# Attention, gated MLP and expert attention on one core: trace durations and nearly equal leanings for the scheduler behind the first attention

## The chip, the cores and the metric

The kernel runs on one core of one Trainium2 chip. The metric is device microseconds of one execution, the median over runs on the chip. TensorE (PE in the profile) multiplies matrices, VectorE (DVE), ScalarE (ACT) and GpSimd (POOL) work element by element, and SyncE (SP) issues transfers.

## The reference

Three parts follow one another, each on the output of the part before (numpy, shortened):

```
# 1: causal attention, 2 batches x 12 heads, 448 rows, 64 wide
attn = softmax(where(mask, -1e9, q @ k.T / 8));  x = attn @ v        # -> (2, 448, 768)
# 2: gated MLP
h = gelu(x @ w_in);  u, v = h[..., :512], h[..., 512:]
v_n = (v - mean) / sqrt(var + 1e-6) * g_ln
v_s = einsum('ts,bsd->btd', w_sg, v_n) + b_sg[None, :, None]
x2 = x + (u * v_s) @ w_out
# 3: four experts, each a causal attention of one head, two of them used per row
w = softmax of the two largest of x2 @ w_gate
for e in range(4):
    q, k, v = x2 @ wq[e], x2 @ wk[e], x2 @ wv[e]
    out += (e chosen) * w_e * (softmax(mask(q @ k.T / 8)) @ v @ wo[e])
```

## The kernel before

Most products are made from values split in two parts, a rounded high part and the remainder (names ending in h and l: gh and gl, xh and xl, wqh and wql). One product is then three matmuls, h by h, l by h and h by l (`mm3`, L820, and `u_chain`, L859). A split is two element-wise steps: a cast or copy that makes the high part (lines L371 on ScalarE, L373 on VectorE, L375 on GpSimd, all in one helper) and a subtraction that makes the remainder (L378, on VectorE or GpSimd). A name such as gl0_3 is the remainder of batch 0, block 3.

The first attention ends near 112 us of the span with the last products with v (L497). Behind it the parts overlap in time. `v_chain` makes v (gelu, layernorm; L990 to L1005), `spatial` multiplies by w_sg (L1053, eight blocks: 2 batches x 4 blocks f of 128 columns) and makes g: scale and bias on VectorE (L1056), the product with u (L1059), then the split into gh and gl. `wout_chain` multiplies g by w_out, 12 matmuls for each of 2 x 6 blocks d, adds x (L1074 the high part, L1077 the low part) and splits the sum into xh and xl. Then come the weights and projections of part 3 (v, then q and k for two pairs of experts in each batch; the pair's results are copied out of the accumulators as q30, k30, q31, k31, L371 or L373). `scores3` (L1302) makes the scores, `bank_chain` (L427, L437, L471, L473) the exponentials and their split as pn, a transposing transfer (L476, issued by SyncE, sixteen in all) turns pn into pt, `out_chain` multiplies pt by the values v3s (L516, L518, L520) and scales the result (r: L531, L533, L536; y: L541 on VectorE in one step, or L543 on ScalarE followed by L547 on GpSimd), `y_split` transposes y (L557) and splits it, and `wo_chain` (L1341) makes the output rows, which leave by transfers.

The order is not written by hand. The class `Order` plans it when the program is built: each part is a chain of steps, a step has a cost in ns for every engine that may do it, and `begin` works out for each engine the time at which the step could start. It picks the engine whose start + cost + leaning is least. The leaning is a constant per engine (`BIAS`; behind planned time 190000 ns `LATE`), to which a kind of step may add its own. `run` then takes, over all chains, the step that starts first, with ties within 60 ns broken by a rank (`R`). The instructions are issued on each engine in the order so planned, and the costs and leanings are nothing but plan: on the chip, an engine does its own instructions in this order, each as soon as what it needs is there. Costs come from the small functions `act` (ScalarE), `mm` (a matmul), `vec` and `vec2` (VectorE), `pool1` and `pool2` (GpSimd), L63 to L82, and from numbers written at single steps (for instance L425, L434, L989, L994, L1002, L1054).

The two lines that decide between engines:

```
bias = self.LATE[e] if t > self.TURN else self.BIAS[e] * min(1.0, t / 20000)
best = (t + c + bias, t, e, t + c)      # the least of these over the engines
```

Of the kernel before, what the change touches and what calls it, by code (L numbers as in the profile page):

```python
# [22 lines left out]
HF = 512  # L23
# [34 lines left out]

def act(n, sb=True, ap=False):
    return (94 if sb else 51) + 93 * ap + n / 1.2


def mm(n):
    return 2 + n / 2.4


def vec(n):
    return 69 + n / 0.96  # L70


def vec2(n):
    return 69 + n / 1.92


def pool1(n):
    return 56 + n / 0.96


def pool2(n):
    return 150 + 2.1 * n  # L82


class Step:
# [25 lines left out]
class Order:  # L111
# [10 lines left out]
    }  # L122

    BIAS = dict(T=0, A=300, V=800, G=-400, S=0, Z=0)
    LATE = dict(T=0, A=300, V=700, G=-300, S=0, Z=0)
    TURN = 190000

    def __init__(self):
        self.clock = dict.fromkeys("TAVGSZ", 600.0)
# [65 lines left out]
    def begin(self, ch):  # L195

        st = ch[4]
        for m in st.need:
            if m not in self.marks:
                return None  # L200
        items = []
        for r in st.take:
            name = r if isinstance(r, str) else r[0]
            free = [x for x in self.rings[name] if not any(x is y for y in items)]
            if not free or (name != r and self.held[r[:2]] + st.take.count(r) > r[2]):
                return None
            items.append(min(free, key=lambda x: x[0]))
        best = None
        for e, c in st.cost.items():

            t = ch[5] if st.dma and ch[3] == "D" else ch[2] + self.delay(ch[3], e)
            t = max(self.clock[e], t)
            for m in st.need:
                t = max(t, self.marks[m][0] + self.delay(self.marks[m][1], e))
            for x in items:
                t = max(t, x[0] + self.delay(x[1], e))
            if st.dma:
                t = max(t, self.hw)
            if e == "T" and not self.warm(t):
                c *= 2  # L220
            bias = self.LATE[e] if t > self.TURN else self.BIAS[e] * min(1.0, t / 20000)
            bias += st.bias.get(e, 0)
            if best is None or t + c + bias < best[0]:
                best = (t + c + bias, t, e, t + c)
        return best[2], best[1], items, best[3]
# [67 lines left out]
def attention_moe_kernel(  # L293
# [19 lines left out]
    o = Order()  # L313
    done, give = o.done, o.give

    uid = [0]

    def nm(s):
# [68 lines left out]
        return dict(A=act(n, False), V=vec(n))  # L387

    def subs(n):
        return dict(V=vec(n), G=pool2(n))  # L390


    class Core:
# [23 lines left out]
    def bank_chain(c, key, bank, s, pts, pt_of=None):  # L417

        parts = []
        for i in BANKS[bank]:  # L420
            _, c0, n = PLACE[i]

            parts.append((i, slice(0, 64 if i == 0 else P), slice(c0, c0 + n)))

        _, tm, bias = yield op(V=690, take=("tm" + c.n, "bias" + c.n))  # L425
        for i, rs, cs in parts:
            V.tensor_tensor_reduce(  # L427
                out=tm[rs, cs], in0=s[rs, cs], in1=masks[i][rs], scale=-0.125, scalar=3.0e38,
                op0=ALU.add, op1=ALU.min, accum_out=bias[rs, i : i + 1],
            )  # L430
        give(BS, s)
        if not c.split:
            _, p32, sm = yield op(A=1000, take=("p32" + c.n, "sm" + c.n))
        else:  # L434
            _, p32 = yield op(A=800, take=("p32" + c.n,))
        for n, (i, rs, cs) in enumerate(parts):
            A.activation(p32[rs, cs], tm[rs, cs], AF.Exp, bias=bias[rs, i : i + 1], scale=-1.0,  # L437
                         **({} if c.split else dict(accum_out=sm[rs, n : n + 1])))
        give("tm" + c.n, tm)
        give("bias" + c.n, bias)  # L440
        if not c.split:
            yield op(G=230)
            G.tensor_scalar(sm[:, 0:2], sm[:, 0:2], 1.0, 1e-9, op0=ALU.mult, op1=ALU.add)
            yield op(V=160)
            V.reciprocal(sm[:, 0:2], sm[:, 0:2])  # L445
            e, = yield op(kind="pr", G=950, V=500)
            for n, (i, rs, cs) in enumerate(parts):
                if e == "V":
                    V.tensor_scalar(p32[rs, cs], p32[rs, cs], sm[rs, n : n + 1], None, op0=ALU.mult)  # L449
                else:  # L450
                    G.tensor_scalar(p32[rs, cs], p32[rs, cs], sm[rs, n : n + 1], 0.0, op0=ALU.mult, op1=ALU.add)  # L451
            give("sm" + c.n, sm)
            _, t = yield op(T=440, take=(BT,))
            for blk, to in enumerate(SLOTS[bank]):
                T.transpose(t[:, to * P : to * P + P], p32[:, blk * P : blk * P + P], ident)  # L455
            give("p32" + c.n, p32)
            pt = yield from pt_of()
            e, = yield Step(copies_ps(512), kind="pt")
            copy(e, pt.rearrange("p (a s) q -> p a s q", s=4)[:, :, 2 * bank : 2 * bank + 2, :],
                 t.rearrange("p (a s q) -> p a s q", a=2, s=2))  # L460
            give(BT, t)
            pts["pt"] = pt
            done(("p", key, bank))
            return
        e, pn = yield Step(copies(512), ("pn" + c.n,), kind="hi")
        if e == "A":
            A.mul(pn[:, :512], p32, PSC)
        elif e == "V":
            V.tensor_scalar(pn[:, :512], p32, PSC, None, op0=ALU.mult)
        else:  # L470
            G.tensor_scalar(pn[:, :512], p32, PSC, 0.0, op0=ALU.mult, op1=ALU.add)  # L471
        yield op(V=vec(512))
        V.scalar_tensor_tensor(pn[:, 512:], p32, PSC, pn[:, :512], op0=ALU.mult, op1=ALU.subtract)  # L473
        give("p32" + c.n, p32)
        _, pt = yield dma_t(896, ("pt" + c.n,))
        nc.sync.dma_start_transpose(pt, pn)  # L476
        give("pn" + c.n, pn)
        pts[bank] = pt
        done(("p", key, bank))
# [446 lines left out]

    def open_c2():
        yield wait(*[("x", b, c) for b in range(B) for c in range(NC)])
        s1_stack.close()
        s3a = ctx.enter_context(tc.tile_pool(name="s3a", bufs=1, side="right"))  # L930
        for c in range(NC):
            wvh.append(ct([P, NV], F32R, f"wvh{c}", s3a))
            wvl.append(ct([P, NV], F32R, f"wvl{c}", s3a))
        c2 = c2_stack.enter_context(tc.tile_pool(name="c2", bufs=1, side="right"))
        for b in range(B):

            vn[b] += [ct([P, HF], F32, f"vn{b}_{j}", c2) for j in range(4)] if b == 0 else []
        vn[1] += [vn[0][0], *[ct([P, HF], F32, f"vn1_{j}", c2) for j in range(1, 4)]]
        for c in range(4):
            wsg.append(ct([P, SG], F32, f"wsg{c}", c2))  # L940

        wsg[0] = [wsg[0], ct([P, SG], F32, "wsg0b", c2)]
        for t, rows in zip(wsg[0], (LOW, TOP)):
            G.memset(t[rows], 0.0)
        u2[1] = [ct([P, S], F32, f"u2_1_{f}", c2) for f in range(4)]
        done("c2")
        for c in range(4):
            o.add(R["sgt"] + c, sg_chain(c))
# [30 lines left out]
    def v_chain(b, j):  # L979
# [6 lines left out]
        _, v2 = yield Step({"Z": 0}, ("big",))  # L986
        yield from gelu2(v2, o_, HF, v2)
        give(BC, o_)
        _, m = yield op(V=602, take=("mv",))  # L989
        V.bn_stats(m[:, 0:6], v2)  # L990
        yield op(V=75)
        V.bn_aggr(m[:, 6:8], m[:, 0:6])

        yield op(G=1120)  # L994
        G.tensor_scalar(m[:, 8:9], m[:, 6:7], -1.0, 0.0, op0=ALU.mult, op1=ALU.add)
        G.tensor_scalar(m[:, 7:8], m[:, 7:8], 1.0, 4e-6, op0=ALU.mult, op1=ALU.add)
        G.tensor_tensor(m[:, 7:8], m[:, 7:8], nhalf, op=ALU.pow)
        G.tensor_mul(m[:, 8:9], m[:, 8:9], m[:, 7:8])
        yield wait("c2")
        e, = yield op(V=456, A=act(HF, ap=True) + 100)  # L1000
        x = vn[b][j]
        if e == "V":  # L1002
            V.tensor_scalar(x, v2, m[:, 6:7], m[:, 7:8], op0=ALU.subtract, op1=ALU.mult)
# [38 lines left out]
    def spatial(b, f):  # L1042
        fs = slice(f * P, f * P + P)

        ts_ = slice(64, SG) if b == 0 else slice(0, S)
        _, t = yield op(T=4 * mm(S), take=(BC,),
                        need=["halves", *[("vn", b, j) for j in range(1, 4)], *[("sg", c) for c in range(4)], ("u", b, f)])
        for j in range(4):
            if j:
                yield op(T=4 * mm(S), need=[("vn", b, 0)] if j == 3 else ())  # L1050

            i, w = (j + 1, wsg[j + 1]) if j < 3 else (0, wsg[0][b])
            T.matmul(t[:, :S], lhsT=vn[b][i][:, fs], rhs=w[:, ts_], start=(j == 0), stop=(j == 3))  # L1053
        _, g0 = yield op(V=596, take=("big",))  # L1054
        g = g0[:, :S]
        V.scalar_tensor_tensor(g, t[:, :S], g_half[:, f : f + 1], b_half[:, ts_], op0=ALU.mult, op1=ALU.add)  # L1056
        give(BC, t)
        e, = yield Step(subs(S))
        (V if e == "V" else G).tensor_mul(g, g, u2[b][f])  # L1059
        done(("gm", b, f))  # L1060
        yield wait("g")
        yield from halves(g, S, gh[b][f], gl[b][f], ("g", b, f))
        give("big", g0)
# [390 lines left out]
```

## Time and profile before

| what | us |
|---|---|
| median of 3 runs (lowest, highest) | 315.57 (314.58, 316.84) |
| the profiled execution | 315.39 |
| its span | 313.3 |
| outside the span | 2.1 |
| PE busy | 295.6 (94%) |
| POOL busy | 211.9 (68%) |
| DVE busy | 194.8 (62%) |
| ACT busy | 169.0 (54%) |

The busy times are averages over parts with different limits. The first attention takes all of the engines; from 112 us on TensorE is nearly always at work, and what can be gained or lost there is its waits. So the views to read are TensorE's waits behind 112 us, with the stretches of its timeline around them, and then the engine that each wait names.

### The profile page before, as it was taken

What the parts mean: (1) busy time and instruction counts of PE and PEld (TensorE: products, weight loads), DVE (VectorE), ACT (ScalarE), POOL (GpSimd) and SP (SyncE); (2) the same over time, 40 slices, a digit from 0 to 9 for tenths busy, and PEclk for the clock granted to TensorE, in tenths of its full rate; (3) what the DMA queues carried; (4) which work ended last, traced back from release to release, by engine and by line L of the source; (5) the groups of instructions that cost most, each with busy time, mean ns of one, the idle gap of its engine ahead of it and who ended that gap; (6) DMA issues with size and microseconds to landing.
All of it is one profiled execution on the core that took longest, in us unless ns stands there. A gap on an engine that the chain in (4) does not pass through costs nothing.

```text
span 313.3 us, 6233 instructions
## 1 busy us (share of the span) xinstructions
PE 295.6 (94%) x2076; PEld 232.5 (74%) x2076; DVE 194.8 (62%) x595; ACT 169.0 (54%) x442; POOL 211.9 (68%) x379
## 2 busy tenths in 40 slices
PE   6799999999999999999999999799979999999894
PEld 6467676766666888897886556699958899887793
DVE  3866876999869756334877842156952561858510
ACT  2778989888989753225664310122213363654543
POOL 4679877797868887546669799889995330463510
PEclk9789999999999999999999999999999999999999
DMA  7999556417101034116333000023210640029846
GB/s 212 205 229 223 129 134 180 116 50 212 67 4 58 13 134 119 34 34 179 71 113 93 19 19 0 0 50 69 69 40 27 121 82 18 1 54 132 154 154 201
DMA packets 55184, 29.91 MB, mean 95 GB/s; under 512 B 42800, under 2 KB 52592, under 8 KB 55152
## 3 DMA queue, kind: packets, MB, share of 16 engines
q1 hardware_dynamic: 55152, 29.52, 39.4%
q8 instruction: 16, 0.26, 0.4%
q14 instruction: 16, 0.13, 0.2%
HBM read 22.43 MB, written 2.75 MB: 80 GB/s over the span
## 4 chain that ended last, share of the span: by engine, by line
PE 44%; POOL 26%; DVE 10%; DMA 10%; issue 5%; ACT 3%; SPq 1%; POOLq 0%; ACTq 0%; DVEq 0%
PE bank L820 16%; PE bank L497 5%; PE bank L859 5%; PE bank L775 4%; POOL xl L378 4%; PE bank L455 4%; PE bank L1341 3%; PE bank L1302 3%; DMA raw<-in_moe_w_in_dram 3%; POOL big L1059 3%; POOL big L1077 2%; POOL gl L378 2%; POOL p L451 2%; DVE p L449 2%; DMA qraw<-in_q_dram 2%
## 5 line engine op out<-in xcount | busy, mean ns | idle before, releaser
L437 ACT ACTIVATE p<-tm,bias 128x192 f32<-128x192 f32 (+3 forms) x128 | 61.9, 504 | 9.6 <-DVE bias L427 9.5
L451 POOL TENSOR_SCALAR p<-p,sm 128x192 f32<-128x192 f32 (+1 forms) x88 | 45.6, 531 | 5.7 <-DVE sm L445 4.9
L427 DVE CUSTOM_DVE_ANT_0 tm<-bank,maskw 128x448 f32<-128x448 f32 (+2 forms) x96 | 39.3, 436 | 1.8 <-ACT p L437 1.3
L775 PE MATMUL bank<-kt,qt 64*128 64x128 f32 (+4 forms) x240 | 32.8, 399 | 2.1 <-ACT kt L371 2.1
L455 PE MATMUL bank<-ident,p 128*128 128x128 f32 x192 | 29.6, 285 | 2.1 <-POOL p L451 1.2
L775 PEld LDWEIGHTS bank<-kt,qt 64*128 64x128 f32 (+1 forms) x240 | 16.8, 193 | 15.2 <-issue 10.5
L371 ACT COPY pt<-bank 128x512 f32<-128x512 f32 x41 | 23.3, 587 | 8.3 <-PE bank L455 8.0
L497 PE MATMUL bank<-pt,v_raw 128*64 128x128 f32 (+3 forms) x336 | 27.4, 315 | 0.0
L455 PEld LDWEIGHTS bank<-ident,p 128*128 128x128 f32 x192 | 20.9, 142 | 8.7 <-POOL p L451 4.6
L497 PEld LDWEIGHTS bank<-pt,v_raw 128*64 128x64 f32 x336 | 19.7, 137 | 8.3 <-issue 5.2
L1053 PE MATMUL bank<-wsg,vn 128*128 128x448 f32 x56 | 21.7, 539 | 0.0
L471 POOL TENSOR_SCALAR pn<-p 128x512 f16<-128x512 f32 x15 | 10.4, 698 | 16.2 <-DMA pt<-pn 9.4
L427 DVE CUSTOM_DVE_ANT_0 tm<-bank,mask 128x192 f32<-128x192 f32 x32 | 11.2, 349 | 16.1 <-PE bank L1302 12.0
L833 DVE TENSOR_TENSOR big<-big,bank 128x448 f32<-128x448 f32 (+1 forms) x15 | 9.7, 652 | 17.5 <-POOL big L831 15.9
L649 DVE SCALAR_TENSOR_TENSOR raw<-raw 128x384 int32<-128x384 int32 (+1 forms) x22 | 15.5, 710 | 5.8 <-POOL raw L647 5.6
L820 PE MATMUL bank<-gh,wuh 128*128 128x448 f32 x48 | 18.1, 377 | 1.0 <-ACT gh L371 1.0
L437 ACT ACTIVATION_READ_ACCUMULATOR p<-tm,bias 128x1 f32 x96 | 18.7, 194 | 0.0
L820 PE MATMUL bank<-gl,wuh 128*128 128x448 f32 x48 | 17.9, 372 | 0.7 <-POOL gl L378 0.5
L1053 PEld LDWEIGHTS bank<-wsg,vn 128*128 128x128 f32 x56 | 10.7, 190 | 10.1 <-issue 9.8
L859 PE MATMUL bank<-xh,wuh 128*128 128x448 f32 x48 | 18.0, 375 | 0.0
L859 PE MATMUL bank<-xl,wuh 128*128 128x448 f32 x48 | 17.8, 371 | 0.0
L859 PE MATMUL bank<-xh,wul 128*128 128x448 f32 x48 | 17.6, 371 | 0.0
(208 smaller groups left out, 837.4 us busy)
## 6 DMA issues: line engine op xcount, KB each, us to landing
raw<-in_moe_w_in_dram SPq DMA_DIRECT2D x8, 384.0 KB, 6.2
raw<-in_moe_w_in_dram SPq DMA_DIRECT2D x6, 512.0 KB, 4.1
raw<-in_moe_w_out_dram SPq DMA_DIRECT2D x8, 384.0 KB, 3.1
qraw<-in_q_dram SPq DMA_DIRECT2D x12, 224.0 KB, 4.5
kraw<-in_k_dram SPq DMA_DIRECT2D x12, 224.0 KB, 4.3
v_raw<-in_v_dram SPq DMA_DIRECT2D x18, 128.0 KB, 4.5
out_dram<-v3r SPq DMA_DIRECT2D x3, 384.0 KB, 3.4
raw<-in_moe_w_sg_dram SPq DMA_DIRECT2D x2, 392.0 KB, 4.0
```

Source lines behind the costliest of these rows:

```text
L371: A.copy(dst, src)
L378: (V if e == "V" else G).tensor_sub(dst, a, b_)
L427: V.tensor_tensor_reduce(out=tm[rs, cs], in0=s[rs, cs], in1=masks[i][rs], scale=-0.125, scalar=3.0e38, op0=ALU.add, op1=ALU.min, accum_out ...
L437: A.activation(p32[rs, cs], tm[rs, cs], AF.Exp, bias=bias[rs, i : i + 1], scale=-1.0, **({} if c.split else dict(accum_out=sm[rs, n : n + ...
L451: G.tensor_scalar(p32[rs, cs], p32[rs, cs], sm[rs, n : n + 1], 0.0, op0=ALU.mult, op1=ALU.add)
L455: T.transpose(t[:, to * P : to * P + P], p32[:, blk * P : blk * P + P], ident)
L497: T.matmul(out_, lhsT=x[:, j, :], rhs=rhs, start=(n == 0), stop=(n == len(FLIPS) - 1), skip_group_check=True)
L649: V.scalar_tensor_tensor(low, low, 29, high, op0=ALU.logical_shift_right, op1=ALU.bitwise_or)
L775: T.matmul(s[:m, c0 + c : c0 + c + n], lhsT=qt[rows, QCOL[i] : QCOL[i] + m], rhs=kt[rows, k0 : k0 + n], start=True, stop=True)
L820: T.matmul(o_, lhsT=a, rhs=b_, start=(i == 0), stop=(i == n - 1))
L859: T.matmul(t[:, :S], lhsT=ks[0][a], rhs=ks[1][b_], start=(c == 0 and i == 0), stop=(c == NC - 1 and i == 2))
L1053: T.matmul(t[:, :S], lhsT=vn[b][i][:, fs], rhs=w[:, ts_], start=(j == 0), stop=(j == 3))
```

## The change

A global `PHASE` is set to 1 when all of the first attention's output is there (in `open_c2`). From then on `at(old, new)` gives the second number: other costs for all the cost functions and for some single steps, and other leanings. `LATE` now counts for the whole of the second phase, with 100 for ScalarE and VectorE and 0 for GpSimd, where the leanings were 300, 800 and -400 (700 and -300 for VectorE and GpSimd behind 190000 ns). The first attention is planned with the old numbers. All lines move down by 7, those behind L940 by 8.

```diff
+PHASE = [0]
+def at(*by_phase):
+    return by_phase[PHASE[0]]
 def act(n, sb=True, ap=False):
-    return (94 if sb else 51) + 93 * ap + n / 1.2
+    return at((94 if sb else 51) + 93 * ap, (193 if sb else 160) + 196 * ap) + n / 1.2
 def mm(n):
-    return 2 + n / 2.4
+    return at(2, 13) + n / 2.4
 def vec(n):
-    return 69 + n / 0.96
+    return at(69, 147) + n / 0.96
 def vec2(n):
-    return 69 + n / 1.92
+    return at(69 + n / 1.92, 130 + n / 1.76)
 def pool1(n):
-    return 56 + n / 0.96
+    return at(56 + n / 0.96, 150 + n / 1.08)
 def pool2(n):
-    return 150 + 2.1 * n
+    return at(150 + 2.1 * n, 200 + 2.12 * n)
...
-    LATE = dict(T=0, A=300, V=700, G=-300, S=0, Z=0)
-    TURN = 190000
+    LATE = dict(T=0, A=100, V=100, G=0, S=0, Z=0)
...
-            bias = self.LATE[e] if t > self.TURN else self.BIAS[e] * min(1.0, t / 20000)
+            bias = self.LATE[e] if PHASE[0] else self.BIAS[e] * min(1.0, t / 20000)
...
     def subs(n):
-        return dict(V=vec(n), G=pool2(n))
+        return dict(V=vec(n) + at(0, 0.3 * n), G=pool2(n))
...
-        _, tm, bias = yield op(V=690, take=("tm" + c.n, "bias" + c.n))
+        _, tm, bias = yield op(V=at(690, 990), take=("tm" + c.n, "bias" + c.n))
...
-            _, p32 = yield op(A=800, take=("p32" + c.n,))
+            _, p32 = yield op(A=at(800, 1010), take=("p32" + c.n,))
...
         yield wait(*[("x", b, c) for b in range(B) for c in range(NC)])
+        PHASE[0] = 1
...
-        _, m = yield op(V=602, take=("mv",))
+        _, m = yield op(V=682, take=("mv",))
...
-        yield op(G=1120)
+        yield op(G=1500)
...
-        e, = yield op(V=456, A=act(HF, ap=True) + 100)
+        e, = yield op(V=500, A=act(HF, ap=True))
...
-        _, g0 = yield op(V=596, take=("big",))
+        _, g0 = yield op(V=684, take=("big",))
```

The numbers of instructions that an engine issues in all change so: GpSimd from 384 to 319, VectorE from 594 to 672, ScalarE from 346 to 327, TensorE (1702 rows) and SyncE (141) stay. Up to the end of the first attention the orders are the same. Three places (the numbers in the names are those of batch, block and buffer):

GpSimd's order in the spatial part before: products with u (L1059), casts (L375) and remainders (L378) of blocks 2 and 3 of batch 0 and the first of batch 1.

```order
L1059 TENSOR_TENSOR big1_117<-big1_117,u2_0_2_114 128x448
L375 TENSOR_SCALAR gh0_2_1991<-big1_117 128x448
L378 TENSOR_TENSOR gl0_2_1992<-big1_117,gh0_2_1991 128x448
L1059 TENSOR_TENSOR big2_118<-big2_118,u2_0_3_115 128x448
L375 TENSOR_SCALAR gh0_3_1993<-big2_118 128x448
L378 TENSOR_TENSOR gl0_3_1994<-big2_118,gh0_3_1993 128x448
L1059 TENSOR_TENSOR big3_119<-big3_119,u2_1_0_1533 128x448
L375 TENSOR_SCALAR gh1_0_1995<-big3_119 128x448
L378 TENSOR_TENSOR gl1_0_1996<-big3_119,gh1_0_1995 128x448
```

Each block is a chain of three steps on GpSimd there. VectorE's order now at blocks 3 of batch 0 and 0 of batch 1 (L1064 was L1056, L1067 was L1059, L380 was L373, L385 was L378).

```order
L1064 SCALAR_TENSOR_TENSOR big3_119<-bank3_96,g_half_87,b_half_58 128x448
L1067 TENSOR_TENSOR big3_119<-big3_119,u2_0_3_115 128x448
L380 CAST gh0_3_1992<-big3_119 128x448
L385 TENSOR_TENSOR gl0_3_1993<-big3_119,gh0_3_1992 128x448
L1064 SCALAR_TENSOR_TENSOR big2_118<-bank7_100,g_half_87,b_half_58 128x448
L1067 TENSOR_TENSOR big2_118<-big2_118,u2_1_0_1533 128x448
L380 CAST gh1_0_1994<-big2_118 128x448
L385 TENSOR_TENSOR gl1_0_1995<-big2_118,gh1_0_1994 128x448
```

All four steps of a block now stand on VectorE one behind the other, for block 3 of batch 0 and the four blocks of batch 1.

GpSimd's order in the x2 part before, blocks 3 to 5 of batch 0 (L1077 adds the low part of x, L375 casts, L378 makes the remainder).

```order
L1077 TENSOR_TENSOR big3_119<-big3_119,xl3_84 128x448
L375 TENSOR_SCALAR xh3_78<-big3_119 128x448
L378 TENSOR_TENSOR xl3_84<-big3_119,xh3_78 128x448
L378 TENSOR_TENSOR xl4_85<-big0_116,xh4_79 128x448
L1077 TENSOR_TENSOR big1_117<-big1_117,xl5_86 128x448
L375 TENSOR_SCALAR xh5_80<-big1_117 128x448
L378 TENSOR_TENSOR xl5_86<-big1_117,xh5_80 128x448
```

GpSimd made every remainder here and two of the three sums.

VectorE's order in the x2 part now, the last two blocks of batch 0 and the first of batch 1 (L1082 was L1074, L1085 was L1077).

```order
L1082 TENSOR_TENSOR big0_116<-bank5_98,xh4_79 128x448
L385 TENSOR_TENSOR xl3_84<-big2_118,xh3_78 128x448
L1085 TENSOR_TENSOR big0_116<-big0_116,xl4_85 128x448
L380 CAST xh4_79<-big0_116 128x448
L1082 TENSOR_TENSOR big1_117<-bank6_99,xh5_80 128x448
L1085 TENSOR_TENSOR big1_117<-big1_117,xl5_86 128x448
L1082 TENSOR_TENSOR big3_119<-bank2_95,xh1_76 128x448
L380 CAST wqh4_2114<-raw0_104 128x256
L385 TENSOR_TENSOR xl5_86<-big1_117,xh5_80 128x448
```

Before, GpSimd did half of the L1077, and most of the casts and remainders of this part were on ScalarE and GpSimd; on VectorE stand now 12 of L1082, 11 of L1085, 10 casts and 7 remainders of x2 blocks, and 4 casts and one remainder of weights; GpSimd keeps 11 remainders of weights of 256 columns, 5 of x2 blocks and one L1085.

TensorE's order in the last part before, around the last scores (k31 by q31) and the transposes of the first y (y330).

```order
L520 MATMUL bank6_99<-v3s0_0_2142,pt33_2455 128x65
L820 MATMUL bank2_95<-xl4_85,wkh4_2128 128x448
L820 MATMUL bank2_95<-xh4_79,wkl4_2134 128x448
L820 MATMUL bank2_95<-xh5_80,wkh5_2129 128x448
L820 MATMUL bank2_95<-xl5_86,wkh5_2129 128x448
L820 MATMUL bank2_95<-xh5_80,wkl5_2135 128x448
L1302 MATMUL bank0_93<-k31_2478,q31_2476 128x128
```

The first value block (L516 to L520) ends right ahead of these rows. TensorE's order now (L1310 was L1302, L827 was L820, L523 to L527 were L516 to L520).

```order
L827 MATMUL bank0_93<-xl5_86,wkh5_2127 128x448
L827 MATMUL bank0_93<-xh5_80,wkl5_2133 128x448
L1310 MATMUL bank2_95<-k31_2472,q31_2470 128x128
L1310 MATMUL bank6_99<-k31_2472,q31_2470 128x128
L1310 MATMUL bank2_95<-k31_2472,q31_2470 128x64
L1310 MATMUL bank6_99<-k31_2472,q31_2470 128x64
L1310 MATMUL bank2_95<-k31_2472,q31_2470 128x320
L1310 MATMUL bank6_99<-k31_2472,q31_2470 128x320
L1310 MATMUL bank5_98<-k31_2472,q31_2470 128x448
L1310 MATMUL bank1_94<-k31_2472,q31_2470 128x448
```

The last projection and the last scores come before the 60 matmuls of the first value block instead of behind them, and the transposes of y330 stand directly behind that block.

## Rows read from the trace of the kernel before

**Rows 1.** Page, part 1: busy us, share and instructions of each engine.
```profile
PE 295.6 (94%) x2076; PEld 232.5 (74%) x2076; DVE 194.8 (62%) x595; ACT 169.0 (54%) x442; POOL 211.9 (68%) x379
```

**Rows 2.** Waits of PE, 112 to 313 us: us in total, times, longest.
```profile
PE bank L820 <- POOL xh L375: 1.4, 1, 1.4
PE bank L820 <- ACT gh L371: 1.0, 1, 1.0
PE bank L516 <- DMA pt<-pn: 0.9, 1, 0.9
...
PE bank L820 <- POOL xl L378: 0.8, 1, 0.8
PE bank L1302 <- ACT k L371: 0.6, 1, 0.6
PE bank L820 <- POOL gl L378: 0.5, 1, 0.5
PE bank L557 <- POOL y L547: 0.4, 1, 0.4
```

**Rows 3.** Timeline of PE at two stops: start us, us, engine, line.
```profile
197.35 0.36 PE L820 MATMUL bank<-gh,wul 128*128 128x448 f32 x1
197.55 0.37 PE L820 MATMUL bank<-gh,wuh 128*128 128x448 f32 x1
...
201.10 0.36 PE L820 MATMUL bank<-gh,wul 128*128 128x448 f32 x1
...
231.24 0.47 PE L820 MATMUL bank<-xl,wqh 128*128 128x448 f32 x1
...
234.85 0.37 PE L820 MATMUL bank<-xh,wql 128*128 128x448 f32 x1
```

**Rows 4.** Chain that ended last, one block of the spatial part.
```profile
186.49 1.10 POOL big L1059
...
189.44 1.10 POOL big L1059
```

**Rows 5.** Timeline of PE, spatial part, start of two blocks, and of the next part.
```profile
185.51 0.92 PE L1053 MATMUL bank<-wsg0b,vn 128*128 128x448 f32 x2
...
188.52 0.92 PE L1053 MATMUL bank<-wsg0b,vn 128*128 128x448 f32 x2
...
191.93 0.71 PE L820 MATMUL bank<-gh,wuh 128*128 128x448 f32 x1
```

**Rows 6.** Groups of DVE by shape: count, busy us, mean ns, idle before.
```profile
L1074 DVE TENSOR_TENSOR big<-bank,xh 128x448 f32<-128x448 f32 x12 | 7.3, 615 | 4.3 <-PE bank L820 4.3
L1056 DVE SCALAR_TENSOR_TENSOR big<-bank,g_half,b_half 128x448 f32<-128x448 f32 x7 | 4.6, 677 | 6.9 <-POOL gl L378 4.5 <-PE bank L1053 2.3
...
L373 DVE CAST wqh<-raw 128x256 fp32r<-128x256 f32 x1 | 1.3, 1255 | 0.0
...
L373 DVE CAST wvh<-raw 128x260 fp32r<-128x260 f32 x1 | 0.3, 297 | 2.7 <-DMA raw<-in_moe_w_gate_dram 2.7
```

**Rows 7.** Timelines of POOL and of DVE, x2 part, 207.5 to 214.6 us.
```profile
207.77 1.35 POOL L378 TENSOR_TENSOR xl<-big,xh 128x448 fp32r<-128x448 f32 x1
...
208.02 1.58 DVE L1077 TENSOR_TENSOR big<-big,xl 128x448 f32<-128x448 f32 x1
...
210.17 0.62 DVE L1077 TENSOR_TENSOR big<-big,xl 128x448 f32<-128x448 f32 x1
```

**Rows 8.** Timelines of the last part: PE, POOL and SP.
```profile
279.81 0.19 PE L520 MATMUL bank<-v3s,pt 128*128 128x65 f16 x1
...
280.95 0.61 POOL L547 TENSOR_TENSOR y<-y,r 128x256 f32<-128x256 f32 x1 [0.30 <-DVE r L536]
281.94 0.62 POOL L471 TENSOR_SCALAR pn<-p 128x512 f16<-128x512 f32 x1 [0.38 <-DMA pt<-pn]
283.29 0.62 POOL L471 TENSOR_SCALAR pn<-p 128x512 f16<-128x512 f32 x1 [0.73 <-DMA pt<-pn]
...
278.66 17.74 SPq L476 DMA_TRANSPOSE pt<-pn  x10
```

More of the change, by code (lines that the diff above doesn't have):

```diff
@@ L314, in attention_moe_kernel @@
     done, give = o.done, o.give
+    PHASE[0] = 0
     uid = [0]
@@ L432, in bank_chain @@
         if not c.split:
-            _, p32, sm = yield op(A=1000, take=("p32" + c.n, "sm" + c.n))
+            _, p32, sm = yield op(A=at(1000, 1400), take=("p32" + c.n, "sm" + c.n))
         else:
-            _, p32 = yield op(A=800, take=("p32" + c.n,))
+            _, p32 = yield op(A=at(800, 1010), take=("p32" + c.n,))
         for n, (i, rs, cs) in enumerate(parts):
```

## The prediction

> **What bounds the kernel now.** I first read the page's busy times: TensorE is busy 94% of the span [rows 1], so the time is TensorE's work plus the places where it waits. Next the list of TensorE's waits behind the first attention (112 us to the end) [rows 2]. The reader is to see that they are few: the seven rows come to 5.6 us, and the largest share names GpSimd or a step behind it (xh 1.4, xl 0.8, gl 0.5, and gh 1.0, where ScalarE waited for GpSimd's product). TensorE's own timeline shows what two of these places really cost [rows 3]: matmuls of 448 columns start 0.20 us apart (197.35, 197.55). From 197.55 to 201.10 there are five starts, which would need 1.0 us and take 3.55: 2.5 us lost. From 231.24 to 234.85 there are four, needing 0.8 and taking 3.6: 2.8 us lost. Together 5.3 us, all of it late operands that GpSimd makes. Why they are late stands in the chain of work that ended last, which runs through GpSimd there: in the spatial part one block f takes it from 186.49 to 189.44, 2.95 us, product, cast and remainder one behind the other [rows 4], while TensorE makes a block in 3.01 us (185.51 to 188.52) [rows 5]. GpSimd just keeps pace, so it never makes good the time it started late, and TensorE meets this at 197.55. The remaining waits lie behind 280 us: a k copy (0.6), a transposed pn (0.9), a y (0.4) [rows 2].
>
> **The change part by part.** The first attention keeps its costs and leanings, and the issue orders are the same up to its end: nothing there, cost 0 from both sides. Behind it the table makes GpSimd no longer the favoured engine: of 384 GpSimd instructions 319 are left, VectorE goes from 594 to 672, ScalarE from 346 to 327. TensorE has the same 1702 rows, so its work is unchanged; what counts is its waits.
>
> (1) *Spatial part.* Products, casts and remainders of the g blocks go to VectorE. Per block VectorE then has L1056 at 0.68 [rows 6], L1059 and gl, each like the uncovered two-input operation of the same size at 0.62 [rows 7], and a cast at between 0.30 (a 260-column one) and 1.26 (a 256-column one, while GpSimd was at work) [rows 6]: 2.2 to 3.2 us against TensorE's 3.01. GpSimd has only mv, wul, two products and one remainder left there, so I take 0.45 for the cast, 2.4 us a block. VectorE ends each block in time, and the last gl is ready about 2.5 us behind its last matmul. TensorE needs it over 5 us behind that (197.35, [rows 3], against 191.93, [rows 5], where the last block's matmuls are through). The first stall goes: -2.5 us. If VectorE took 3.2 us instead, it would fall 0.2 us behind a block, 1.4 over seven, still inside the 2.5 us of cover.
>
> (2) *x2 part.* VectorE gets 12 x L1074, 11 x L1077, 8 remainders and 14 casts in a window of 12 chains of 12 matmuls at 0.20 us, some 30 us. Light end: 12 x 0.615 + 19 x 0.62 + 14 x 0.30 = 23.4 us [rows 6, 7]. Heavy end: every one of the other 33 steps at 1.4, between the cast at 1.26 and L1077 at 1.58 beside a GpSimd instruction [rows 6, 7]: 7.4 + 33 x 1.4 = 53.6 us. GpSimd keeps 6 remainders and products at 1.35 and 11 of 256 columns (about 0.77, by columns), 16.6 us of 30, so a VectorE step meets one about half of the time and waits for about half of it, 0.5 us: 33 x 0.5 x 0.5 = 8, in all 31.4 us. Behind the last chain TensorE still has 29 matmuls of the v projection (0.12 each by their 260 columns) and 15 of q, 6.5 us, before it needs the last xh and xl of the first batch; the last block's own four steps take about 3. So VectorE may have 33.5 us in the window, and 31.4 fits with 2 us to spare. The second stall goes: -2.8 us. Its cover is those 2 us. From VectorE work of 36.3 us on, the stall is as large as before.
>
> What the trace shows on this sharing: L1077 on VectorE took 1.58 us when it began inside GpSimd's xl (207.77 to 209.12), and 0.62 at 210.17 [rows 7]. The Trainium skill, "SBUF — State Buffer", section "Who interferes with whom", says that a VectorE instruction with two SBUF inputs and a GpSimd instruction that reads SBUF exclude each other, whoever starts first; "Perfetto Trace Analysis", section "Optimizing Scalar/DVE Operations", draws from the shared port that offloading between the two might not help. The rows agree with the exclusion. By the second sentence moving work from GpSimd to VectorE would give nothing here; by the rows the moved product itself drops from 1.10 on GpSimd [rows 4] to 0.62 on VectorE [rows 7], so the sum of both falls. What that sentence comes to, worked out from rows, is the first rival below.
>
> (3) *Projections and gates.* The orders are nearly equal, and TensorE has no wait there but the k copies. With k or q copies on VectorE behind pn steps the wait of 0.6 can grow by 0 to 0.5; I take +0.2.
>
> (4) *The end.* The last k projection and the last scores now stand ahead of the first value block (60 small matmuls of L516 to L520), and the transpose of y (L557) directly behind it. In the trace of before the last small matmul starts at 279.81 and y is ready at 281.56 (280.95 + 0.61) [rows 8], 1.75 us later, with projections and scores in between. Now TensorE would wait for that chain with nothing between: ScalarE's r, VectorE's reciprocal, product and y. Bounds 1.2 (y on VectorE instead of GpSimd) to 2.5 (behind a pn step); I take +1.9. Against that, scores that come earlier let exponentials, pn and transposes start earlier. The ten last transposes take 17.74 us, 1.77 each [rows 8], while the steps that wait for one another on them show 1.35 us as the pace (281.94 to 283.29) [rows 8]. So the transposes can come several us earlier, and the waits for pt and y behind 289 (0.9 + 0.4, [rows 2]) may go, between 0 and -1.3; I take -0.7. Two more output matmuls (384 columns, 0.17 each by the 0.20 for 448) stand behind the last value block: +0.35.
>
> Sum: -2.5 - 2.8 + 0.2 + 1.9 - 0.7 + 0.35 = -3.5 us. The profiled execution took 315.39 us (span 313.3, 2.1 around it), 0.2 under the median of 315.57. 315.4 - 3.5 = 311.9 us.
>
> **Rivals.**
> First rival, slower: VectorE becomes the bound of the x2 part through the sharing shown in [rows 7]. For it: its new work is of the kinds that were seen at 1.26 and 1.58 us. Against: GpSimd is only half as full as before. Price: with VectorE at 40 us (between 31.4 and 53.6) the wait at 231 is 40 - 33.5 = 6.5 instead of 2.8, +3.7; the first stall still goes (-2.5); the end costs +1.9 + 0.35 + 0.2 with no earlier transposes to pay for it: +3.6, 319.0 us. It decides from 36.3 us of VectorE work: there the second stall is unchanged, and what the first gives back (2.5) the end takes (2.45).
>
> Second rival, no change: the gain of 5.3 us is lost in the end, because transposes set the last value block. For it: the DMA queue takes 10 of them in 17.74 us, at whatever time TensorE arrives, and the wait for y is new. Against: the pace of 1.35 shows that they are not at the queue's limit. Price: -5.3 + 1.9 + 0.35 + 0.2 + 1.9 (the waits for pt grow by what TensorE is still ahead, less 1) = about -1, 314.4 us.
>
> Third rival, more: all GpSimd-made waits go, y is ready without a wait because TensorE's blocks give VectorE room, and the transposes run at 1.35: 9 x (1.77 - 1.35) = 3.8 us earlier on top of the head start of which TensorE can use what it idled, 1.3. -5.3 - 1.3 + 0.35 - 0.6 (k copies) = -6.9, 308.5 us.
>
> Fourth: the change doesn't do what it says, since its durations are of operations alone and the contended ones differ; then stalls only change places, 315 us.
>
> **How the numbers follow.** Forecast 0.45, its own range 310.3 to 313.5 from the bounds of (3) and (4); first rival 0.17 (316 to 321); second 0.18; third 0.18; fourth 0.02. A measurement of this kernel can tell about 1% from no change, so the bounds are 312.4 and 318.7. Two thirds of the forecast lie under 312.4 (0.30), with the third rival 0.48 faster. The rest of the forecast 0.15, most of the second rival 0.15, a part of the first 0.05 and the fourth 0.02 make 0.37 for no change. Slower: 0.12 of the first, 0.03 of the second, 0.15. The range for 8 in 10 takes in the third rival and the near half of the first: 307.5 to 318.0.
>
> **What would show it.** Right: no wait of TensorE in L820 for gl, gh, xh, xl; GpSimd no longer full from 180 to 235; VectorE's L1077 mean under 0.9; TensorE at the scores 7 us earlier than before, then a wait of some 2 us at L557. Wrong in (2): a wait in L820 for a VectorE step at the q projection of 2 us or more, with VectorE busy over 95% from 200 to 225. Wrong in (4): a wait at L557 under 1 us, or waits for pt that add up to more than 2 us. The whole is wrong if TensorE's waits behind 112 us come to more than before.

## The result, and the profile after

| | before | after |
|---|---|---|
| median, us (lowest, highest), 6 runs each | 315.81 (314.58, 318.88) | 312.40 (311.16, 313.71) |
| the profiled execution, us | 315.39 | 313.71 |
| its span, us | 313.3 | 311.9 |

The ratio is 0.988, with a 95% interval of 0.984 to 0.992: the kernel is faster by 1.2%, 3.4 us. The forecast was 311.9 us, -3.5.

The busy times on the page of the changed kernel, to be held against [rows 1]:

```profile
PE 294.0 (94%) x2076; PEld 234.0 (75%) x2076; DVE 227.4 (73%) x673; ACT 162.4 (52%) x423; POOL 162.8 (52%) x314
```

GpSimd is busy for 49 us less and ScalarE for 7 us less, and VectorE for 33 us more, with the same steps in all. TensorE's waits behind the first attention, which answer to [rows 2] (line, what it waited for, us in total, times, longest):

```profile
PE bank L523 <- DMA pt<-pn: 3.3, 3, 2.5
PE bank L564 <- DVE y L548: 1.8, 2, 1.6
PE bank L1310 <- DVE k L380: 0.8, 1, 0.8
PE bank L976 <- DVE wvnl L385: 0.6, 1, 0.6
```

All waits for operands of the g and x2 blocks are gone (L827 is the L820 of before), and so is GpSimd as a releaser. In their place the waits for pt have grown from 0.9 to 3.3 us and those for y from 0.4 to 1.8. At the places of the two stops in [rows 3], the products of the g blocks and the first q projection, TensorE's timeline now reads:

```profile
199.09 0.37 PE L827 MATMUL bank<-gh,wuh 128*128 128x448 f32 x1
199.29 0.36 PE L827 MATMUL bank<-gl,wuh 128*128 128x448 f32 x1
...
228.09 0.36 PE L827 MATMUL bank<-xh,wql 128*128 128x448 f32 x1
228.29 0.36 PE L827 MATMUL bank<-xh,wqh 128*128 128x448 f32 x1
228.49 0.36 PE L827 MATMUL bank<-xl,wqh 128*128 128x448 f32 x1
```

A start every 0.20 us, with nothing lost at either. VectorE's groups of the x2 part (178 to 238 us), which answer to [rows 6] and the sum made of them:

```profile
L1085 DVE TENSOR_TENSOR big<-big,xl 128x448 f32<-128x448 f32 x11 | 10.1, 915 | 0.2
L1082 DVE TENSOR_TENSOR big<-bank,xh 128x448 f32<-128x448 f32 x12 | 7.4, 617 | 1.1 <-PE bank L827 1.1
L380 DVE CAST xh<-big 128x448 fp32r<-128x448 f32 x10 | 5.6, 561 | 0.3
L385 DVE TENSOR_TENSOR xl<-big,xh 128x448 fp32r<-128x448 f32 x7 | 5.0, 707 | 0.1
...
L380 DVE CAST wkh<-raw 128x256 fp32r<-128x256 f32 x3 | 1.4, 466 | 0.0
...
L380 DVE CAST wqh<-raw 128x256 fp32r<-128x256 f32 x1 | 0.8, 818 | 0.6 <-DMA raw<-in_moe_wq_dram 0.6
```

They add up to 30.3 us, one remainder of a weight (0.4) aside. GpSimd, 9.7 of 10 us at work from 220 to 230 before, is down to 3.9 there, while VectorE is at 9.7:

```profile
220.00:230.00 10.00, 10.00 (x63) 9.56 (x62) 9.66 (x17) 0.79 (x2) 3.92 (x6) 1.00 0.07 16
```

(from - to and length in us; busy us and instructions of TensorE, its weight loads, VectorE, ScalarE and GpSimd; then the granted clock as a share of full speed, DMA share and GB/s.)

**Where the time went.** The two profiled executions differ by 1.7 us, the medians by 3.4. The first attention, whose orders are the same, happened to end 1.74 us later in the execution of after, so everything behind it is counted from its last product with v. The starts are those of TensorE's rows in the two timelines; the row for the last scores counts to the first of them:

| from - to | before, us | after, us | difference |
|---|---|---|---|
| last product with v (112.60; 114.34) - first spatial matmul | 55.6 | 55.4 | -0.2 |
| spatial part | 23.7 | 23.7 | 0.0 |
| w_out blocks, v, first q and k, to the first scores | 47.6 | 41.3 | -6.3 |
| first scores - last scores | 42.2 | 41.0 | -1.2 |
| last scores - last output matmul | 26.8 | 32.1 | +5.4 |
| last output matmul - end of span | 4.8 | 4.0 | -0.8 |
| outside the span | 2.1 | 1.8 | -0.3 |

The sum is -3.4, as large as the difference of the medians. Of the -6.3 some 0.6 is order (five matmuls of the v projection now stand behind the first scores), and of the -1.2 and +5.4, 1.8 is the first value block, which moved from ahead of the last scores to behind them. Cleared of that: -5.8 us up to the last scores, +3.5 behind them, -1.1 after the last matmul.

One reading lesson: the lists of TensorE's waits come to 6.6 us before and 6.5 after, and by them alone nothing would have been gained, while the last output matmul came 2.3 us earlier. In this trace an idle gap is shorter than what a stop costs, as a row of the first stop before shows:

```profile
198.44 0.47 PE L820 MATMUL bank<-gl,wuh 128*128 128x448 f32 x1 [0.52 <-POOL gl L378]
```

The matmul ahead of it starts at 197.55 and is shown for 0.37 us [rows 3], though like matmuls start 0.20 us apart. The gap of 0.52 counts from the end of that record; by the starts 0.89 - 0.20 = 0.69 us were lost. Starts of like matmuls against their usual distance tell more.

### The profile page after: what moved, and what is told of

The parts are those of the page before. It is cut to its first block, busy times and chain, and to the rows that moved or that the text cites. A ratio compares the mean times of both kernels' runs of the same rounds, so it can differ in the third digit from the quotient of the medians.

```text
span 311.9 us, 6208 instructions
## 1 busy us (share of the span) xinstructions
PE 294.0 (94%) x2076; PEld 234.0 (75%) x2076; DVE 227.4 (73%) x673; ACT 162.4 (52%) x423; POOL 162.8 (52%) x314
## 4 chain that ended last, share of the span: by engine, by line
PE 72%; DMA 10%; DVE 8%; POOL 5%; issue 3%; ACT 1%; SPq 1%; DVEq 0%; ACTq 0%; POOLq 0%
PE bank L827 33%; PE bank L1061 8%; PE bank L504 6%; PE bank L782 5%; PE bank L866 5%; PE bank L1349 4%; PE bank L462 4%; DMA raw<-in_moe_w_in_dram 3%; PE bank L1310 3%; DMA pt<-pn 3%; POOL p L458 2%; DVE p L456 2%; DMA qraw<-in_q_dram 2%; PE bank L737 2%; DMA b_half<-in_moe_b_sg_dram 2%
## 5 line engine op out<-in xcount | busy, mean ns | idle before, releaser
L378 ACT COPY pt<-bank 128x512 f32<-128x512 f32 x41 | 23.3, 587 | 9.5 <-PE bank L462 9.1
L478 POOL TENSOR_SCALAR pn<-p 128x512 f16<-128x512 f32 x10 | 6.8, 678 | 33.6 <-ACT p L444 28.9
L656 DVE SCALAR_TENSOR_TENSOR raw<-raw 128x384 int32<-128x384 int32 (+1 forms) x22 | 15.1, 687 | 6.2 <-POOL raw L654 6.0
L434 DVE CUSTOM_DVE_ANT_0 tm<-bank,mask 128x192 f32<-128x192 f32 x32 | 11.2, 351 | 10.1 <-PE bank L1310 6.3
L651 ACT ACTIVATE w<-raw 128x384 f32<-128x384 f32 (+1 forms) x22 | 13.0, 589 | 10.3 <-DMA raw<-in_moe_w_in_dram 6.3
L1061 PEld LDWEIGHTS bank<-wsg,vn 128*128 128x128 f32 x56 | 10.6, 190 | 10.1 <-issue 9.7
L827 PE MATMUL bank<-gh,wuh 128*128 128x448 f32 x48 | 17.9, 372 | 0.0
L654 POOL TENSOR_SCALAR raw<-raw 128x384 f32<-128x384 f32 (+1 forms) x22 | 13.3, 606 | 8.3 <-ACT w L651 7.7
```

Source lines behind the costliest of these rows:

```text
L378: A.copy(dst, src)
L434: V.tensor_tensor_reduce(out=tm[rs, cs], in0=s[rs, cs], in1=masks[i][rs], scale=-0.125, scalar=3.0e38, op0=ALU.add, op1=ALU.min, accum_out ...
L654: G.tensor_scalar(f32(high), f32(high), 0.0, 1.0, op0=ALU.mult, op1=ALU.mult)
L656: V.scalar_tensor_tensor(low, low, 29, high, op0=ALU.logical_shift_right, op1=ALU.bitwise_or)
L827: T.matmul(o_, lhsT=a, rhs=b_, start=(i == 0), stop=(i == n - 1))
```

## Experiments

Each kernel was run beside the kernel before. Ratios are to it, with 95% intervals; times are medians. The median of the kernel before lay between 315.8 and 317.2 us from one set of runs to the next, so kernels of different sets are compared by their ratios. A last product with v, a first value block and an end of the span were read in every trace, since the first attention's end varies by 2.7 us between these executions:

| kernel | ratio | us | first value block behind the last product with v | end of span behind the first value block |
|---|---|---|---|---|
| before | | 315.8 | 165.4 | 35.3 |
| after | 0.988 (0.984 to 0.992) | 312.4 | 163.7 | 33.9 |
| dur_only | 1.001 (0.999 to 1.004) | 316.5 | 165.4 | 35.0 |
| lean_only | 0.979 (0.974 to 0.984) | 309.4 | 160.4 | 34.5 |
| new_till_x2 | 0.979 (0.975 to 0.983) | 309.6 | 159.1 | 36.2 |
| new_from_x2 | 1.010 (1.005 to 1.016) | 320.3 | 170.2 | 34.3 |
| early_o | 0.973 (0.967 to 0.980) | 308.4 | 153.3 | 39.7 |
| pt10 | 0.973 (0.968 to 0.978) | 308.6 | 163.4 | 31.1 |
| early_lean_only | 0.969 (0.964 to 0.975) | 307.7 | 153.9 | 39.2 |
| early_before | 0.999 (0.995 to 1.003) | 315.8 | 160.6 | 38.7 |
| lean_only_pt10 | 0.971 (0.965 to 0.977) | 307.4 | 163.6 | 29.0 |
| early_lean_only_pt10 | 0.975 (0.968 to 0.983) | 308.9 | 153.3 | 39.4 |

### Durations alone: dur_only

```diff
-            bias = self.LATE[e] if PHASE[0] else self.BIAS[e] * min(1.0, t / 20000)
+            bias = (dict(A=300, V=700, G=-300).get(e, 0) if t > 190000 else self.BIAS[e] * min(1.0, t / 20000))
```

> New durations, old leanings in the whole plan. GpSimd keeps 7 of the 8 products with u, 7 remainders gl and 11 of 12 remainders xl, as before. Theory (the gain is the two stalls of 5.3 us, and the leanings remove them): both stalls are there, 315 to 317 us, within 1% of before; TensorE's list names GpSimd in L827 with 2 us or more. Rival (the measured durations give the better order): about 312.5 us, as the whole change.

Measured: no difference. Its list of TensorE's waits:

```profile
PE bank L523 <- DMA pt<-pn: 2.7, 3, 2.3
PE bank L827 <- POOL xl L385: 1.5, 2, 0.8
PE bank L827 <- POOL xh L382: 1.2, 1, 1.2
PE bank L564 <- POOL y L554: 0.8, 1, 0.8
PE bank L1310 <- ACT k L378: 0.6, 1, 0.6
```

The wait at the q projection is there with GpSimd as its releaser (2.7 us); of the two stops the first, at the g blocks, is not. So the new durations alone removed that one, and the gain was lost again in the end, where the waits for pt come to 2.7 us against 0.9 and the first value block stands behind the last scores, as in the whole change (the table further down has the two parts). The forecast that both stops stay was wrong in that detail; the time was as forecast.

### Leanings alone: lean_only

```diff
 def at(*by_phase):
-    return by_phase[PHASE[0]]
+    return by_phase[0]
...
-        _, g0 = yield op(V=684, take=("big",))
+        _, g0 = yield op(V=596, take=("big",))
```

(and the other three single steps back to their old numbers in the same way.)

> Old durations, new leanings behind the first attention. All products, remainders and casts of g and x2 blocks go to VectorE and ScalarE, none to GpSimd. Theory: no wait in L827 for operands of the g and x2 blocks, 310.5 to 313 us, as fast as the whole change within 1%. Rival (VectorE becomes the bound of the x2 part, 12 sums, 12 low parts, 12 remainders and 10 casts): a wait for a VectorE step at the q projection of 2 to 6 us, 314 to 318 us.

Measured: faster than before by 2.1%, and than the whole change by 1%, somewhat better than forecast. VectorE's groups of the x2 part:

```profile
L1085 DVE TENSOR_TENSOR big<-big,xl 128x448 f32<-128x448 f32 x12 | 7.5, 629 | 0.2
L385 DVE TENSOR_TENSOR xl<-big,xh 128x448 fp32r<-128x448 f32 x12 | 7.5, 622 | 0.2
```

VectorE does 12 low parts and 12 remainders here against 11 and 7, and needs 15.0 us for them where it needed 15.1 (10.1 + 5.0). GpSimd has no x2 step left in this kernel, and a low part takes 0.63 instead of 0.92 us. In the kernel before, VectorE did six low parts, at 1.20 us each:

```profile
L1077 DVE TENSOR_TENSOR big<-big,xl 128x448 f32<-128x448 f32 x6 | 7.2, 1204 | 0.2
```

The stretch from 180 to 235 us in the kernels before, after and lean_only (columns as in the row of 220 to 230 us above; the fifth busy time is GpSimd's):

```profile
180.00:235.00 55.00, 51.13 (x230) 40.30 (x229) 28.67 (x41) 9.63 (x22) 51.18 (x69) 1.00 0.14 35
180.00:235.00 55.00, 55.00 (x255) 45.19 (x254) 47.03 (x82) 7.05 (x17) 26.90 (x42) 1.00 0.16 39
180.00:235.00 55.00, 55.00 (x258) 45.21 (x259) 45.69 (x93) 6.66 (x16) 10.66 (x28) 1.00 0.15 37
```

GpSimd is at work for 51.2, 26.9 and 10.7 of the 55 us, and the low part on VectorE takes 1.20, 0.92 and 0.63 us. That is the sharing of [rows 7] read the other way: a step that stays on GpSimd costs VectorE time as well. No wait for a VectorE step stands at the projections, so the first rival falls with more work on VectorE than in the change itself.

### The change up to the x2 blocks, or from there on: new_till_x2, new_from_x2

```diff
+    def turn(n):
+        yield wait(*[("x2", b, d) for b in range(B) for d in range(NC)])
+        PHASE[0] = n
...
+    o.add(0, turn(0))
```

`turn` waits for all x2 blocks to be planned and then sets the phase. In new_from_x2 the call is turn(1), and open_c2 leaves PHASE at 0. Phase 0 has all old numbers and leanings in both.

> New durations and leanings from the end of the first attention until the last x2 block is planned, the old ones behind it. Theory: the stalls of 5.3 us go and the end keeps the order of before, with the first value block not behind the last scores: 310 to 311.5 us, 1 to 2 us faster than the whole change. Rival (the gain comes from the end of the program): 314.5 to 316 us.

> Old durations and leanings until the last x2 block is planned, the new ones behind it. Theory: both stalls (5.3 us) stay, and the end waits for y and for transposes as in the whole change: 316.5 to 318.5 us, slower than before by up to 1%. Rival (the gain comes from the end): 312 to 313 us.

Measured: 309.6 and 320.3 us. The part up to the x2 blocks is worth -2.1%, the part behind them costs +1.0%; together -1.1%, and the whole change gave -1.2%. Both lie outside their forecasts, the gain a little (310 to 311.5) and the cost somewhat more (316.5 to 318.5). The list of new_from_x2 has the old stops and the new ones:

```profile
PE bank L524 <- DMA pt<-pn: 1.6, 2, 1.0
PE bank L565 <- DVE y L549: 1.6, 1, 1.6
PE bank L828 <- POOL xh L383: 1.4, 1, 1.4
PE bank L828 <- ACT gh L379: 1.0, 1, 1.0
PE bank L828 <- POOL xl L386: 0.9, 1, 0.9
```

TensorE's starts put each gain and loss in its place. In this table the first value block (1.8 us) is counted behind the last scores in every kernel; differences are to before:

| kernel | the first value block stands | last product with v to the last scores, us | last scores to the last output matmul, us |
|---|---|---|---|
| before | ahead of the last scores | 167.3 | 28.6 |
| after | behind them | 161.5 (-5.8) | 32.1 (+3.5) |
| dur_only | behind them | 164.3 (-3.0) | 32.3 (+3.7) |
| lean_only | ahead of them | 160.5 (-6.8) | 30.4 (+1.8) |
| new_till_x2 | ahead of them | 160.9 (-6.3) | 29.1 (+0.5) |
| new_from_x2 | behind them | 168.0 (+0.7) | 32.8 (+4.2) |

The block stands behind the last scores in the three kernels whose end is planned with the new durations, and ahead of them in the three whose end is planned with the old ones; new leanings alone (lean_only) leave it ahead. So it is the new durations that moved it, and the end costs 3.5 to 4.2 us where it moved and 0.5 to 1.8 where it didn't. Up to the last scores the durations alone gain 3.0 us and the leanings alone 6.8.

### What the loss in the end comes from: early_o, pt10

The last attention has six pt buffers. Six transposes are made early and fill them; the seventh needs a buffer that a value block gives back. In SyncE's list of waits from 260 to 300 us, after:

```profile
SPq L483 <- DVE pn L480: 13.5, 5, 10.5
SPq L483 <- PE bank L527: 11.8, 5, 8.9
```

and before:

```profile
SPq L476 <- DVE pn L473: 12.8, 4, 10.4
SPq L476 <- PE bank L520: 7.1, 4, 4.6
```

The transposes wait for the value blocks for 11.8 us in all, up to 8.9 at once, against 7.1 and 4.6. In the timeline of SyncE of after (start, us until the last is issued), which answers to the last row of [rows 8]:

```profile
278.65 17.16 SPq L483 DMA_TRANSPOSE pt<-pn  x10
```

The first of the ten starts at 278.65 us as it did before (278.66), though the last scores came 5.9 us earlier in the same count (275.79 against 281.72): it follows the first value block, which starts at 277.99 (278.00 before). Counted from the last product with v, the last scores came 7.7 us earlier, block and transpose 1.7. Two edits test this.

early_o puts the first value block ahead of the last projection and scores. In the plan it stands behind them because the values of batch 0 are prepared after those of batch 1; two ranks are exchanged, the later blocks of batch 0 are ranked behind that projection, and each batch gets a diagonal tile (dg) of its own (lines shortened at the dots, the tile's allocation left out):

```diff
-    ... vp=(569.5, 557.4), ...
+    ... vp=(557.4, 569.5), ...
...
-                o.add(R['S'][2 * b + pe] + i + R['av3'], head3(...))
+                o.add(R['S'][2 * b + pe] + i + R['av3'] + 17 * ((b, pe) == (0, 1)), head3(...))
...
-        dg = vabs.bitcast(F32).rearrange("p h j d -> p (h j d)")[:, :P]
+        dg = st["dg"][0 if am is st["v3am"][0] else 1]
```

> The changed kernel with the values of batch 0 prepared before those of batch 1 (two ranks exchanged, a diagonal tile of its own for each batch, the later value blocks ranked behind the last projection), so that the first value block (L523 to L527) stands ahead of the last k projection and scores. In all six kernels read so far the span ended 34 to 36 us behind the first value block. Theory (the transposes from the seventh on wait for the pt buffers that this block frees, so its place sets the end): the first block starts 5 to 7 us earlier and the time falls to 306 to 308.5 us. Rival (the transposes are bound by the queue or by late pn): the first block comes earlier, the end does not, 311.5 to 313 us, with longer waits for pt.

pt10 leaves all ranks and gives ten buffers:

```diff
-        st["core"] = Core(ctx, "left", "3", 3, 3, 6)
+        st["core"] = Core(ctx, "left", "3", 3, 3, 10)
```

> The changed kernel with ten pt buffers for the last attention in place of six; the first value block stays behind the last projection and scores. Theory (pt buffers tie the transposes to the first value block): the seventh to tenth transposes are issued before the first value block, the span ends less than 33 us behind it, 307 to 310.5 us. Rival (queue or pn): the seventh transposes are issued as late as before and the time stays at 311.5 to 313 us.

Measured: 308.4 and 308.6 us, both some 4 us faster than the change. In early_o the first value block came 10.4 us earlier, more than the 5 to 7 of the forecast. Two edits of quite different kinds, one of the block's place and one of the number of buffers alone, give the same, and no wait for pt is left in either list. Neither changes the release of the buffers alone: with transposes planned earlier the planner also orders the end anew (in pt10 two value blocks follow each other), and the waits for y fall from 1.8 us to 0.6 (pt10) and 1.5 (early_o). The list of pt10 from 240 us on:

```profile
PE bank L525 <- POOL v3s L617: 1.7, 1, 1.7
PE bank L1310 <- ACT k L378: 0.6, 1, 0.6
PE bank L564 <- DVE y L548: 0.4, 1, 0.4
PE bank L564 <- POOL y L554: 0.2, 1, 0.2
```

and of early_o:

```profile
PE bank L564 <- DVE y L548: 0.9, 1, 0.9
PE bank L1311 <- ACT k L378: 0.6, 1, 0.6
PE bank L564 <- POOL y L554: 0.6, 1, 0.6
PE bank L523 <- DVE y3l L569: 0.4, 1, 0.4
```

In SyncE's timeline of pt10 eight transposes are issued by 255 us and the other eight from 269.75, the first of them well ahead of the first value block (276.51):

```profile
238.41 16.22 SPq L483 DMA_TRANSPOSE pt<-pn  x8
...
269.75 19.34 SPq L483 DMA_TRANSPOSE pt<-pn  x8
```

How long SyncE waits tells nothing by itself: in early_o its waits for value blocks from 260 to 300 us are as long as in the change (12.1 us, up to 8.9), but the ten transposes start at 266.95 instead of 278.65, and TensorE waits for none.

The 34 to 36 us from the first value block to the end, common to the six kernels first read, are no law: with ten buffers it is 31, with an early block 40.

### How far that goes: early_lean_only, early_before, lean_only_pt10, early_lean_only_pt10

The edits are those above on lean_only and on the kernel before.

> Old durations and new leanings (309.4 us) with the early first value block of the run above. Theory: another 3 to 5 us, 304.5 to 307 us. Rival (the end is bound elsewhere): 308.5 to 310 us.

> The kernel before with the early first value block alone. Theory: the two stalls stay, the end comes 3 to 6 us earlier, 310 to 313 us. Rival (in the kernel before the end is set by what waits for the stalls, not by the value block): 315 to 317 us.

> Old durations, new leanings (309.4 us) with ten pt buffers for the last attention. Theory (what was left of TensorE's waits for pt, 1.7 us in that run's list, goes with the buffers): 306.5 to 308.5 us. Rival (the buffers help only the plan that has the first value block late): 309 to 310 us.

> Old durations, new leanings, early first value block (307.7 us) and ten pt buffers. Theory: with the block early the buffers are free early, so more of them change nothing: 307 to 308.5 us. Rival (the last transposes still wait for buffers): 304 to 306.5 us.

Measured: 307.7, 315.8, 307.4 and 308.9 us. early_before is a miss: the first value block starts 4.8 us earlier (160.6 against 165.4 behind the last product with v) and the time is the same. Its ten last transposes start 4.8 us earlier too. The last scores come 1.3 us later (170.4 against 169.1), but that is order: 90 small value matmuls and four transposes of y stand ahead of them, where there were 60 and none. TensorE's one wait for pt (0.9 us) is gone, and its waits for y and for y's split have grown from 0.4 to 1.6. So in the kernel before the early transposes were worth no more than that wait, and the moved block cost as much; with the change, which brought the scores forward and left the block behind, the waits for pt were 3.3. The kernel before with ten buffers was not run. early_lean_only gained 1.7 us where 3 to 5 were expected, and ten buffers on top of that nothing (its interval overlaps). The best kernels, early_lean_only and lean_only_pt10, are 1.5 to 2% faster than the change and 3% faster than the kernel before; the two can't be told apart, and the intervals of early_o, pt10 and early_lean_only_pt10 overlap with theirs.

## Why the prediction was right, point by point

The time, the sign and the main mechanism were right; one step was wrong by 2 us, and smaller things made up for it. That the number came within 0.5 us of the median is in part luck.

**(1) and (2), the two stops, -2.5 and -2.8: right.** Both are gone, and up to the last scores TensorE gained 5.8 us, the k copy included. In the spatial part a block was put at 2.4 us of VectorE and took 2.35 (189.08 to 191.43), and the last remainder gl ends at 196.44, 3.0 us behind the last spatial matmul where 2.5 were put:

```profile
189.08 0.68 DVE L1064 SCALAR_TENSOR_TENSOR big<-bank,g_half,b_half 128x448 f32<-128x448 f32 x1
...
191.43 0.68 DVE L1064 SCALAR_TENSOR_TENSOR big<-bank,g_half,b_half 128x448 f32<-128x448 f32 x1
...
195.82 0.62 DVE L385 TENSOR_TENSOR gl<-big,gh 128x448 fp32r<-128x448 f32 x1
```

The VectorE work of the x2 part was put at 31.4 us and came to 30.7 (30.3 + 0.4), so the estimate of waiting half of the time for half a GpSimd step held in sum: casts at 0.56 and L1085 at 0.92 lie between the ends taken from [rows 6] and [rows 7]. new_till_x2 shows that this part alone is worth more than the whole change. Most of it comes from the leanings: up to the last scores they gain 6.8 us alone (lean_only), the durations 3.0 (dur_only), and the durations lose theirs again in the end.

**(3), the k copy, +0.2: right.** The wait for k grew from 0.6 to 0.8, and it now names VectorE.

**(4), the end: the wait for y and the output matmuls right, the transposes wrong.** Behind the last value block stand 51 output matmuls instead of 49, as the +0.35 had it. The wait at L564 was put at 1.9 and is 1.8 by the starts (the last small matmul of the first block starts at 279.80):

```profile
281.59 0.66 PE L564 MATMUL bank<-ident,y 128*128 128x128 f32 x4 [1.60 <-DVE y L548]
```

The step that failed is "scores that come earlier let exponentials, pn and transposes start earlier", with its -0.7. It was the scores that were followed, and not what releases a transpose: a pt buffer. The moved value block gives the buffers back, and it came 1.7 us earlier where the last scores came 7.7. The waits for pt grew by 2.4 us instead of shrinking, and the part behind the last scores cost 3.5 us where the steps had 1.9 - 0.7 + 0.35 = 1.55.

**What made up for it:** 0.7 us more than forecast up to the last scores (5.8 where -2.5 - 2.8 + 0.2 makes 5.1), and 1.1 us behind the last output matmul and outside of the span, which no step had. The last matmul to the end took 4.8 us in the profile of before and 4.0 in that of after, and between 3.8 and 5.2 in the other kernels; one profile of each doesn't settle whether the change has a part in it, and it was not tried.

**The signs.** No wait for gl, gh, xh or xl is left, GpSimd is at work for 26.9 of the 55 us from 180 to 235, the last scores are 7.7 us earlier (5.8 without the value block), and the wait at L564 is there; L1085's mean of 0.92 just missed the 0.9. Of the signs of being wrong, waits for pt above 2 us came (3.3), which is the failed step. VectorE was busy for 24.0 of the 25 us from 200 to 225, over the 95% named in (2), but the wait that was to go with it is not there.

**The rivals.** The first (VectorE as the bound) had the right mechanism, the sharing, and the wrong size; lean_only shows that it is GpSimd's share that makes VectorE slow. By "Perfetto Trace Analysis" of the Trainium skill, section "Optimizing Scalar/DVE Operations", offloading between the two engines might not help. Here moving steps from GpSimd to VectorE does help: the two-input steps of g and x2 took 1.19 to 1.29 us on GpSimd before and take 0.62 to 0.63 on VectorE in lean_only, where GpSimd has none of them. The second rival (the gain lost in the end through the transposes) had the loss nearly right: 1.9 + 0.35 + 1.9 = 4.15 behind the last scores, measured 3.5. Its reason, the queue, was not the right one: with ten buffers (pt10) TensorE waits for no transpose at the same queue. Its 314.4 us was wrong since it had nothing of what made up for the loss. The third (more than 5 us) is what early_o and pt10 reach in time with one further edit.

## What to carry to other kernels

Where a step on one engine grows with the work of another, as VectorE's low part did here (0.63, 0.92 and 1.20 us with GpSimd at work for 19, 49 and 93% of the stretch), look at what it costs on each engine alone and beside the other, and try giving the faster engine all of it, until that engine holds up the bound. When work is brought forward on the bounding engine, look in the list of the queue behind it for what releases its buffers; a ring of buffers that is given back by a step which was moved back can set the end, however early the operands are. A change that turns two tables at once should be run with each of them alone, and by halves of the program.

## What was not expected

VectorE took over in 33 us what GpSimd and ScalarE were rid of in 49 and 7. All x2 low parts and remainders on VectorE (24 of them) took as long as 18 of them beside GpSimd, 15.0 against 15.1 us. And planning costs taken from the trace were worth nothing in sum, 316.5 against 316.5 us, and cost the whole change its end: they are what moved the first value block.
